# Turning b1's gradient ahead of the weight gradients, storing du later, and loading two tables behind more of w2: one change to a planned forward and backward kernel

## The chip, the cores and the metric

The kernel runs on one core of a Trainium2 chip. The metric is device time in microseconds; a run's time is that of its one core. The profile shows one execution, so every duration in it is a single sample.

## The reference

One layer of a token mixer and its gradients. With x of 2048 tokens by 448 channels:

```python
def _A_ref(x, w_r, w_i):                       # mixer
    X = rfft2(x) * (w_r + 1j * w_i)
    return irfft2(X, s=(S, D)).astype(bfloat16)

def _B_ref(x, w1, b1, w2, b2):                 # MLP over the tokens
    h = layernorm(x)
    u = gelu(einsum("bsd,sf->bdf", h, w1) + b1)
    return (einsum("bdf,fs->bds", u, w2) + b2).transpose(0, 2, 1)

h  = x + _A_ref(layernorm(x), w_r, w_i)
h2 = h + _B_ref(layernorm(h), w1, b1, w2, b2)
```

The outputs are h2 (out_0) and, for a given grad_out, the gradients of x (out_1), w_r and w_i (out_2, out_3), w1 (out_4, 2048x1792), b1 (out_5, 1792), w2 (out_6, 1792x2048) and b2 (out_7). S is 2048, D 448, F 1792; everything large is bf16.

## The kernel before

The kernel is written as a list of operations and ordered by a planner (class `Plan`). Each operation names the tiles it reads and writes, the engines that may run it with a planned duration, and, for a load, its place in SP's queue. `Plan.order` simulates the engines in time: at each step it takes the engine that can start earliest, and on it the ready operation with the highest priority. Priority is the longest chain of planned durations behind an operation, plus a boost (`pl.boost`, kept as `level`). An operation that may run on two engines goes to the one that is free first. Loads and stores pass through one modelled DMA server. The result is a fixed order per engine, and on the chip each engine runs its own list in order, waiting for semaphores.

The matrix products' banks are one ring of 8, with a limit per kind of use: "mm" 4, "mg" 2, "sp" 5, "sb" 4, "mw" 8, "mp" 6. A bank is taken when its first operation is placed, and comes free when the last reader is through.

The stages in order of time, with the names that the tiles have in the profile:

- Forward FFT over tokens and channels (`fft_rows`, `fft_cols`, banks `ps_sp`), the product with w (`cmul`), and the inverse (`ifft_cols`, `ifft_rows`). `ifft_cols` reads the table `hi`, of which VectorE first makes a negated part (L672); `ifft_rows` reads `di` and `kinv`.
- As filler between these, grad_out by w2 transposed: 14 blocks `w2T`, 16 matmuls each (`ps_mg<-go_n,w2T`), left in `du`. Blocks 0 and 1 of w2 are loaded plain and turned on TensorE (`turn`, L592), eight tiles to a bank, and copied out by ScalarE or VectorE, whichever the planner chooses; the others are loaded by a transposing DMA. The `w2T` tiles share the ring "w4" of five buffers.
- The products with w1 (`ps_mp<-hln,w1c`), 14 blocks of 16 matmuls. For each block ScalarE and VectorE make the GELU and its derivative; `gT` is the GELU, `du` becomes the gradient ahead of it, and `gb1` takes du's sums, one column per block. After every four blocks (L1103), gT and du are stored to `gT_d` and `du_d` in DRAM, from which they are later read back transposed. Stores go through GpSimd's queue.
- out_0: gT by w2 (`ps_mp<-gT,w2c`), boosted by 130.
- du by w1 transposed (`ps_mm<-du,w1T`), 16 blocks of 14 matmuls, each followed by `norm_back`. Meanwhile SP loads `g_t` and `goT` transposed (`ld_t4`: one load for the last 64+64 columns, one or two for the rest, and a copy within the tile through GpSimd's queue), then `w_b` (w again), `xr`, `hlnT` and `du_t`. `du_t` takes over du's place (X8).
- Backward FFT (`ps_sb`), with the gradient of w2 as filler: `outer("mm", g_t, goT, ...)`, 14 blocks of 16 matmuls, each with four banks of kind "mm". One block is: two groups `whole(0)` and `whole(1)` of three matmuls into one bank each, the `tails`, four matmuls on half the rows that touch all four banks, and `whole(2)` and `whole(3)`. Its four evictions on ScalarE (`s<-ps_mm`) are given priority 300.
- The gradient of w1, `outer` with hlnT and du_t: the first 6 of 16 blocks as filler in "mm" banks, the rest in "mw".
- b1's gradient at the end of the list: `gb1b` is gb1 cast to bf16, turned on TensorE (L1372) into a bank of kind "mm", copied out as `gb1r` and stored. It has no boost. Where it lands in time is the planner's choice.

SP's queue in the first stage, in order: x, the FFT's tables, w2 blocks 0 to 3, w_t (four loads), `hi`, `kinv`, `di`, `b1r`, `b2r`, then w2T 4 to 9, w1.

Of the kernel before, what the change touches and what calls it, by code (L numbers as in the profile page):

```python
# [12 lines left out]
BF16 = mybir.dt.bfloat16  # L13
# [5 lines left out]
P = 128  # L19
# [364 lines left out]
def on_act(n, base=0.045):  # L384
    return [("ACT", *_act(n, base))]
# [28 lines left out]
def kernel(  # L414
# [97 lines left out]
    def copy(alts, out, in_, r, w):  # L512
        def go(e, on):
            if on == "ACT":
                e.copy(out=out(), in_=in_())  # L515
            else:
                e.tensor_copy(out=out(), in_=in_())  # L517

        pl.op(alts, go, r=r, w=w)
# [32 lines left out]
    w2T = {}  # L552
    w2n = {}

    def ld_x(g):
        for i in range(4):
            pass
        sl = slice(4 * g, 4 * g + 4)
        ld_parts(x, range(4 * g, 4 * g + 4), lambda b: b[:, sl, :], xv[:, sl, :], P * 4 * D * 2)

    def ld_parts(dst, parts, out, in_, size, transpose=False, r=(), rate=None):
        place[0] += 1
        order = place[0]
        rate = rate or (0.195 if transpose else 0.335)

        def go(e, on):
            kw = {"transpose": True} if transpose else {}
            e.dma_start(out=out(dst), in_=in_() if callable(in_) else in_, **kw)

        pl.op([("SP", 0.45, 0.45)], go, r=r, w=[(dst, k) for k in parts], dma=(size, rate * 1e6, transpose), order=order)  # L570
# [15 lines left out]
    def turn(j, w2n):  # L586
        for a in range(0, NT, 8):
            pt = bank(sp[0], [P, 8, P], BF16)

            def go(e, on, a=a, pt=pt):  # L590
                for t in range(8):
                    e.transpose(pt[:, t], w2n[:, (a + t) * P:(a + t + 1) * P], ident[:])  # L592

            pl.op(mm(*[128] * 8), go, r=[w2n, ident], w=[pt])
            copy(on_act(1024) + [("DVE", 1.13, 1.21)], lambda a=a: w2T[j][:, a:a + 8, :], lambda pt=pt: pt[:], [pt], [(w2T[j], a)])
            turned.append(pl.ops[-1])

    turned = []
# [27 lines left out]
    ld_w2T(3)  # L626
    w_t = big(4, [P, 2, NJ, DF], "w_t")
    ld_w(w_t)
    hi = const("hi", [P, NJ, 3, 64])
    ld(hi, lambda b: b[:, :, 1:3, :], hnd["hi"].ap(), P * NJ * 2 * 64 * 2, w=(hi, 0))  # L630
    kinv = table("kinv", "kinv", [P, 3, P])
    di0 = table("di0", "di", [P, 2, 2, DC])
    b1r = const("b1r", [NFB, P])
    ld(b1r, lambda b: b[:], B_b1.rearrange("(j p) -> j p", p=P), 4000)
    b2r = const("b2r", [NT, P])
    ld(b2r, lambda b: b[:], B_b2.rearrange("(t p) -> t p", p=P), 4000)
    ld_w2T(4)
    ld_w2T(5)
    ld_w2T(6)
    ld_w2T(7)  # L640
    ld_w2T(8)
# [428 lines left out]
    for j in range(NFB):  # L1070
        wc, o = w1c[j]
        pu = product("mp", D, [(lambda wc=wc, o=o, h=h: wc[:, h, o:o + P], lambda h=h: hln[:, h, :],
                                [(wc, j), (hln, h)]) for h in range(NT)], [P, 512])
        ge = pl.buf("e4", [P, 4, D], "ge")
        uf, q_, zz, hh = 0, 1, 2, 3
        kk = zz

        def gop(alts, r, w, fn, ge=ge):
            pl.op(alts, lambda e, on: fn(e, lambda i: ge[:, i, :]), r=[(ge, k) if isinstance(k, int) else k for k in r],
                  w=[(ge, k) if isinstance(k, int) else k for k in w])  # L1080

        gop([("ACT", 0.516, 0.62)], [pu, b1c], [uf], lambda e, g, j=j, pu=pu: e.activation(
            out=g(uf), in_=pu[:, 0:D], func=ACT.Identity, bias=b1c[:, j:j + 1]))
        gop([("ACT", 0.516, 0.62)], [pu, b1q], [q_], lambda e, g, j=j, pu=pu: e.activation(  # L1084
            out=g(q_), in_=pu[:, 0:D], func=ACT.Square, bias=b1q[:, j:j + 1], scale=Q6))
        gop(stt, [q_, uf], [zz], lambda e, g: e.scalar_tensor_tensor(  # L1086
            out=g(zz), in0=g(q_), scalar=6.0 * GELU_C, in1=g(uf), op0=ALU.add, op1=ALU.mult))
        gop([("ACT", 0.475, 0.57)], [zz], [hh], lambda e, g: e.activation(
            out=g(hh), in_=g(zz), func=ACT.Sigmoid, scale=1.0 / 3.0))
        gop(bf_tt, [uf, hh], [(gT, j)], lambda e, g, j=j: e.tensor_tensor(  # L1090
            out=gT[:, j, :], in0=g(uf), in1=g(hh), op=ALU.mult))
        gop([("ACT", 0.475, 0.57)], [zz], [kk], lambda e, g: e.activation(
            out=g(kk), in_=g(zz), func=ACT.Sigmoid, scale=-1.0 / 3.0))
        gop(stt, [q_, uf], [q_], lambda e, g: e.scalar_tensor_tensor(
            out=g(q_), in0=g(q_), scalar=2.0 * GELU_C, in1=g(uf), op0=ALU.add, op1=ALU.mult))
        gop(bf_tt, [kk, q_], [kk], lambda e, g: e.tensor_tensor(out=g(kk), in0=g(kk), in1=g(q_), op=ALU.mult))
        gop(bf_tt, [hh, (du, j)], [hh], lambda e, g, j=j: e.tensor_tensor(
            out=g(hh), in0=g(hh), in1=du[:, j, 0:D], op=ALU.mult))
        gop([("DVE", 0.545, 0.69)], [kk, hh], [(du, j), (gb1, j)], lambda e, g, j=j: e.scalar_tensor_tensor(
            out=du[:, j, 0:D], in0=g(kk), scalar=1.0, in1=g(hh), op0=ALU.add, op1=ALU.mult,  # L1100
            accum_out=gb1[:, j:j + 1]))
        copy(small(), lambda j=j: du[:, j, D:D + 1], lambda j=j: gb1[:, j:j + 1], [(gb1, j)], [(du, (j, 1))])
        if j % 4 == 3 or j == NFB - 1:  # L1103
            j0 = j - j % 4
            js = range(j0, j + 1)
            st(lambda j0=j0, j=j: gT_v()[:, j0:j + 1, :], lambda j0=j0, j=j: gT[:, j0:j + 1, :],
               P * len(js) * D * 2, [(gT, k) for k in js], [(gT_d, j)])
            st(lambda j0=j0, j=j: du_v()[:, j0:j + 1, :], lambda j0=j0, j=j: du[:, j0:j + 1, 0:D],
               P * len(js) * D * 2, [(du, k) for k in js], [(du_d, j)])

# [70 lines left out]

    def norm_back(pb, xhat, xkey, h, nm, base, out, okey):


        nm2 = col(1, "nm2", bufs=3)
        ab = col(2, "nm1", bufs=3)  # L1190
        junk = pl.buf("jk", [P, D], "junk")
        v = pl.buf("f2", [P, D], "v", F32)

        def total(src, key, scale, r):
            pl.op([("DVE", 0.605, 0.73)], lambda e, on: e.tensor_tensor_reduce(  # L1195
                out=junk[:], in0=src[:, 0:D], in1=xhat(), scale=scale(), scalar=0.0, op0=ALU.mult,
                op1=ALU.add, accum_out=nm2[:]), r=[key, xkey] + r, w=[junk, nm2])

        def scaled():
            pl.op([("ACT", 0.53, 0.64)], lambda e, on: e.activation(  # L1200
                out=v[:], in_=pb[:, 0:D], func=ACT.Identity, scale=nm.rn[:, h, 0:1], bias=ab[:, 1:2]),
                r=[pb, ab, (nm.rn, (h, 0))], w=[v])

        if nm.rneg is not None:
            by, m = lambda: ab[:, 0:1], ab
            total(pb, pb, lambda: nm.rneg[:, h:h + 1], [nm.rneg])
            pl.op([("DVE", 0.075, 0.17)], lambda e, on: e.tensor_scalar(  # L1207
                out=ab[:], in0=nm.rn[:, h, :], scalar1=nm2[:], scalar2=None, op0=ALU.mult),
                r=[nm2, (nm.rn, (h, 0)), (nm.rn, (h, 1))], w=[ab])
            scaled()  # L1210
        else:
            by, m = lambda: nm2[:], nm2
            pl.op([("DVE", 0.131, 0.213)], lambda e, on: e.tensor_scalar(  # L1213
                out=ab[:, 1:2], in0=pb[:, D:D + 1], scalar1=nm.rn[:, h, 0:1], scalar2=-1.0 / D, op0=ALU.mult,
                op1=ALU.mult), r=[pb, (nm.rn, (h, 0))], w=[ab])
            scaled()
            total(v, v, lambda: nm.back, [])
        pl.op([("DVE", 0.595, 0.68)], lambda e, on: e.scalar_tensor_tensor(  # L1218
            out=junk[:], in0=xhat(), scalar=by(), in1=v[:], op0=ALU.mult, op1=ALU.add),
            r=[xkey, m, v, junk], w=[junk])  # L1220
        pl.op(tt(448), lambda e, on: e.tensor_tensor(out=out(), in0=junk[:], in1=base(), op=ALU.add),  # L1221
              r=[junk, okey[0]], w=[okey[1]])
# [14 lines left out]
    for h in range(8, NT):  # L1237
        ld_w1T(h)
        if h == 11:
            ld_t4(g_t, lambda: gT_d[:], [gT_d])  # L1240
    ld_t4(goT, lambda: grad_out[0], [], 2)
    dh = go_r
    for h in range(NT):
        pd = product("mm", D + 1, [(lambda h=h, j=j: w1T[h][0][:, w1T[h][1], j, :], lambda j=j: du[:, j, 0:D + 1],
# [121 lines left out]

    gb1b = const("gb1b", [P, NFB])
    copy(small(), lambda: gb1b[:], lambda: gb1[:], [gb1], [gb1b])  # L1370
    pt1 = bank("mm", [NFB, P], BF16)
    pl.op(mm(128), lambda e, on: e.transpose(pt1[:], gb1b[:], ident[:]), r=[gb1b, ident], w=[pt1])  # L1372
    gb1r = const2("b1r", [NFB, P], "gb1r")
    copy(small(), lambda: gb1r[:], lambda: pt1[:], [pt1], [gb1r])
    st(out_5.rearrange("(j p) -> j p", p=P), lambda: gb1r[:], 4000, [gb1r])
    gb2b = const("gb2b", [P, NT])
    copy(small(), lambda: gb2b[:], lambda: gb2[:], [gb2], [gb2b])
    st(out_7.rearrange("(q h) -> q h", h=NT), lambda: gb2b[:], 4000, [gb2b])
# [33 lines left out]
```

## Time and profile before

| | |
|---|---|
| median of 3 runs | 346.82 us (345.92 to 347.43) |
| the profiled execution | 345.45 us, span 343.7 us |
| granted TensorE clock | 0.997 |
| TensorE, matmul | busy 325.3 us (95%), 2507 instructions |
| TensorE, weight load | busy 174.3 us (51%) |
| VectorE | busy 269.1 us (78%) |
| ScalarE | busy 194.3 us (57%) |
| GpSimd | busy 70.9 us (21%), nearly all of it DMA issues |
| DMA | 80.98 MB, mean 236 GB/s |

The profiled execution's own time is its span and 1.75 us around it. Matmuls are pipelined and their ends are modelled, so short pauses of TensorE can hide in "busy". A bracket behind a line of the timeline gives the engine's idle time just before, and who ended it. ps_ names are banks, by kind.

### The profile page before, as it was taken

Reading aid. Unit: us, or ns where it says so; the run is one execution under the profiler, and the core shown is the slowest. Engines: PE = TensorE matmul, PEld = TensorE weight load, DVE = VectorE, ACT = ScalarE, POOL = GpSimd, SP = SyncE. Lnnn points to the kernel's source line nnn. Section 1 sums busy time; section 2 is a strip of 40 time slices with the busy share of each in tenths; the row PEclk is TensorE's granted clock in tenths of the full one; section 3 lists DMA queues with packets and bytes.
Section 4 is the critical chain, followed back from the end, with each engine's and each line's share of the span. In section 5 each row is a group of like instructions: output and inputs, shape, how many; then the busy total and the mean of one; then the engine's idle time right before and its main releaser. Section 6 shows DMA issues by size and latency. Waiting matters only on the chain. (4 is left out here: it accounts for less than half of the span.)

```text
span 343.7 us, 6872 instructions
## 1 busy us (share of the span) xinstructions
PE 325.3 (95%) x2507; PEld 174.3 (51%) x2507; DVE 269.1 (78%) x756; ACT 194.3 (57%) x416; POOL 70.9 (21%) x125
## 2 busy tenths in 40 slices
PE   0979999999999999999999999889999999999994
PEld 0546555666655555555555555544445655544441
DVE  5898999897649997060267887869999799999773
ACT  2897833476568773616012322687876888665332
POOL 0000000056520101040340000010111133336553
PEclk9999999999999999999999999999999999999998
DMA  7999699979799999899969999999999466556756
GB/s 255 383 241 209 143 189 260 221 202 292 216 333 262 355 306 317 249 331 244 217 121 269 201 212 232 240 203 199 211 200 200 181 232 230 196 201 215 254 202 201
DMA packets 134845, 80.98 MB, mean 236 GB/s; under 512 B 94332, under 2 KB 127228, under 8 KB 134684
## 3 DMA queue, kind: packets, MB, share of 16 engines
q1 hardware_dynamic: 127180, 52.71, 71.4%
q0 software_dynamic: 7632, 27.84, 22.7%
q8 instruction: 19, 0.31, 0.5%
q14 instruction: 14, 0.11, 0.1%
HBM read 30.98 MB, written 27.08 MB: 169 GB/s over the span
## 5 line engine op out<-in xcount | busy, mean ns | idle before, releaser
L525 PE MATMUL ps_mg<-go_n,w2T 128*128 128x448 bf16 x224 | 49.9, 355 | 1.6 <-DMA go_n<-in_grad_out_dram 0.8
L525 PE MATMUL ps_mm<-goT,g_t 128*128 128x512 bf16 (+1 forms) x224 | 50.4, 380 | 0.4 <-DVE zt L517 0.4
L515 ACT CAST s<-ps_mm 128x512 bf16<-128x512 f32 (+1 forms) x72 | 38.8, 584 | 8.2 <-PE ps_mm L525 7.5
L525 PE MATMUL ps_mm<-du,w1T 128*128 128x449 bf16 x224 | 43.3, 353 | 0.0
L525 PE MATMUL ps_mp<-hln,w1c 128*128 128x448 bf16 x224 | 43.0, 352 | 0.0
L525 PE MATMUL ps_mp<-gT,w2c 128*128 128x448 bf16 x224 | 42.7, 352 | 0.0
L1200 ACT ACTIVATE v<-ps_mm,nm,rn_h 128x448 f32<-128x448 f32 x16 | 11.6, 724 | 43.9 <-DVE nm L1213 43.9
L525 PEld LDWEIGHTS <-w1T 128*128 128x128 bf16 x224 | 21.8, 97 | 21.1
L525 PEld LDWEIGHTS <-w2c 128*128 128x128 bf16 x224 | 21.9, 98 | 20.5
L525 PEld LDWEIGHTS <-w1c 128*128 128x128 bf16 x224 | 21.8, 98 | 20.1
L525 PEld LDWEIGHTS <-hlnT 128*128 128x128 bf16 (+1 forms) x256 | 19.9, 97 | 23.6 <-issue 7.8
L507 POOL DMA_DIRECT2D out_dram<-s x31 | 17.0, 547 | 54.2 <-ACT s L515 34.7
L525 PEld LDWEIGHTS <-w2T 128*128 128x128 bf16 x224 | 19.3, 98 | 17.3 <-issue 1.7
L525 PE MATMUL ps_mw<-du_t,hlnT 128*128 128x448 bf16 (+1 forms) x160 | 27.7, 353 | 0.0
L525 PEld LDWEIGHTS <-g_t 128*128 128x128 bf16 (+1 forms) x224 | 15.4, 96 | 20.1 <-issue 8.5
L1173 DVE SCALAR_TENSOR_TENSOR h<-ps_mp,b2c,hr 128x448 bf16<-128x448 f32 x16 | 9.9, 676 | 19.8 <-PE ps_mp L525 19.8
L515 ACT CAST s<-ps_mw 128x448 bf16<-128x448 f32 x21 | 10.7, 534 | 16.3 <-PE ps_mw L525 12.2
L1086 DVE SCALAR_TENSOR_TENSOR ge<-ge 128x448 bf16<-128x448 bf16 x14 | 8.7, 619 | 14.0 <-ACT ge L1084 14.0
L525 PE MATMUL ps_mm<-du_t,hlnT 128*128 128x448 bf16 (+1 forms) x96 | 18.0, 353 | 0.0
L525 PEld LDWEIGHTS <-kinv 128*128 128x128 bf16 x192 | 14.6, 97 | 6.4 <-DVE eo L951 2.4
L1180 ACT ACTIVATE gb2j<-go_r 128x448 bf16<-128x448 bf16 x16 | 9.2, 576 | 15.0 <-DMA go_r<-in_grad_out_dram 14.6
L507 POOL DMA_DIRECT2D hn_d<-x x4 | 2.4, 599 | 73.0 <-DVE mv_h L719 73.0
(148 smaller groups left out, 602.4 us busy)
## 6 DMA issues: line engine op xcount, KB each, us to landing
w2c<-in_B_w_dram SPq DMA_DIRECT2D x8, 896.0 KB, 8.8
out_dram<-s POOLq DMA_DIRECT2D x14, 512.0 KB, 5.9
out_dram<-s POOLq DMA_DIRECT2D x15, 448.0 KB, 2.9
w1c<-in_B_w_dram SPq DMA_DIRECT2D x6, 1024.0 KB, 10.0
x<-in_A_x_dram SPq DMA_DIRECT2D x4, 448.0 KB, 6.6
go_n<-in_grad_out_dram SPq DMA_DIRECT2D x2, 896.0 KB, 10.3
hn_d<-x POOLq DMA_DIRECT2D x4, 448.0 KB, 6.2
hln_d<-hln POOLq DMA_DIRECT2D x4, 448.0 KB, 6.1
```

The lines of the kernel that those rows point to most:

```text
L507: e.dma_start(out=out() if callable(out) else out, in_=in_())
L515: e.copy(out=out(), in_=in_())
L525: e.matmul(out(), lhsT=lhsT(), rhs=rhs(), start=start, stop=stop)
L1086: gop(stt, [q_, uf], [zz], lambda e, g: e.scalar_tensor_tensor(out=g(zz), in0=g(q_), scalar=6.0 * GELU_C, in1=g(uf), op0=ALU.add, op1=ALU. ...
L1173: pl.op([("DVE", 0.595, 0.68)], lambda e, on, t=t, p2=p2, h2=h2: e.scalar_tensor_tensor(out=h2[:], in0=p2[:, 0:D], scalar=b2c[:, t:t + 1], ...
L1180: pl.op([("ACT", 0.70, 0.80)], lambda e, on, h=h: e.activation(out=gb2j[:], in_=go_r[:, h, :], func=ACT.Copy, accum_out=gb2[:, h:h + 1]), ...
L1200: pl.op([("ACT", 0.53, 0.64)], lambda e, on: e.activation(out=v[:], in_=pb[:, 0:D], func=ACT.Identity, scale=nm.rn[:, h, 0:1], bias=ab[:, ...
```

## The change

Four edits, and one line that only rewrites `ld_x` (the same four loads).

1. The four operations for b1's gradient move from the end of the list to the place behind out_0 and b2's sums, with a boost of 130, and the bank's kind becomes "mg".
2. du's four stores leave the GELU loop and stand behind the loads of goT; each is made to wait for the last of those loads. `pl.ops[-2]` is that load: the last operation of `ld_t4` is the copy within the tile.
3. On SP, w2T 4 goes ahead of kinv, di, b1r and b2r, and `hi` goes behind w2T 5.
4. The planned duration of VectorE's copy of a turned block of w2 goes from 1.13 (to completion 1.21) to 0.62 (0.70). ScalarE's stays at 0.92.

```diff
-            copy(on_act(1024) + [("DVE", 1.13, 1.21)], lambda a=a: w2T[j][:, a:a + 8, :], ...
+            copy(on_act(1024) + [("DVE", 0.62, 0.70)], lambda a=a: w2T[j][:, a:a + 8, :], ...
...
     ld_w(w_t)
-    hi = const("hi", [P, NJ, 3, 64])
-    ld(hi, lambda b: b[:, :, 1:3, :], hnd["hi"].ap(), P * NJ * 2 * 64 * 2, w=(hi, 0))
+    ld_w2T(4)
     kinv = table("kinv", "kinv", [P, 3, P])
...
-    ld_w2T(4)
     ld_w2T(5)
+    hi = const("hi", [P, NJ, 3, 64])
+    ld(hi, lambda b: b[:, :, 1:3, :], hnd["hi"].ap(), P * NJ * 2 * 64 * 2, w=(hi, 0))
     ld_w2T(6)
...
-            st(lambda j0=j0, j=j: du_v()[:, j0:j + 1, :], lambda j0=j0, j=j: du[:, j0:j + 1, 0:D],
-               P * len(js) * D * 2, [(du, k) for k in js], [(du_d, j)])
...
+    pl.boost = 130.0
+    gb1b = const("gb1b", [P, NFB])
+    copy(small(), lambda: gb1b[:], lambda: gb1[:], [gb1], [gb1b])
+    pt1 = bank("mg", [NFB, P], BF16)
+    pl.op(mm(128), lambda e, on: e.transpose(pt1[:], gb1b[:], ident[:]), r=[gb1b, ident], w=[pt1])
+    gb1r = const2("b1r", [NFB, P], "gb1r")
+    copy(small(), lambda: gb1r[:], lambda: pt1[:], [pt1], [gb1r])
+    st(out_5.rearrange("(j p) -> j p", p=P), lambda: gb1r[:], 4000, [gb1r])
+    pl.boost = 0.0
...
     ld_t4(goT, lambda: grad_out[0], [], 2)
+    behind = pl.ops[-2]
+    for j0 in (0, 4, 8, 12):
+        js = range(j0, min(j0 + 4, NFB))
+        st(lambda js=js: du_v()[:, js[0]:js[-1] + 1, :], lambda js=js: du[:, js[0]:js[-1] + 1, 0:D],
+           P * len(js) * D * 2, [(du, k) for k in js], [(du_d, js[0])])
+        pl.ops[-1].deps.add(behind.idx)
...
-    gb1b = const("gb1b", [P, NFB])
...
-    pt1 = bank("mm", [NFB, P], BF16)
...
```

## The prediction

> **What bounds the kernel now.** I read the page first. TensorE is busy for 95% of the span at full granted clock, and its slices show no hole between the first two and the last that a tenth would reveal, apart from one stretch past the middle.
>
> ```profile
> PE 325.3 (95%) x2507; PEld 174.3 (51%) x2507; DVE 269.1 (78%) x756; ACT 194.3 (57%) x416; POOL 70.9 (21%) x125
> ...
> PE   0979999999999999999999999889999999999994
> ...
> DMA  7999699979799999899969999999999466556756
> ```
>
> So a change pays where TensorE stands still, or where its own instructions become fewer. This change removes no arithmetic. I therefore listed the idle time of TensorE by stretches (first number in each line: width; second: TensorE busy). Of 18.4 us idle in the span, 8.0 lie ahead of the first operand, some 5 after the last matmul, 2.6 between 8 and 30 us, and 2.9 in one place, 218 to 226 us:
>
> ```profile
> 214.00:218.00 4.00, 4.00 (x31) 2.34 (x30) 2.57 (x8) 1.16 (x3) 0.00 (x0) 1.00 1.12 259
> 218.00:222.00 4.00, 3.06 (x31) 1.86 (x28) 3.96 (x11) 3.13 (x7) 0.00 (x0) 1.00 1.01 233
> 222.00:226.00 4.00, 2.07 (x32) 1.92 (x32) 3.34 (x12) 3.42 (x8) 0.52 (x1) 1.00 0.99 213
> 226.00:230.00 4.00, 4.00 (x50) 1.99 (x48) 2.04 (x6) 3.58 (x10) 0.57 (x1) 1.00 1.20 250
> ```
>
> The timeline of that place shows why (columns: start, duration, engine, line, operation, and in brackets the idle time before it and who ended it):
>
> ```profile
> 218.35 0.22 PE L1372 MATMUL ps_mm<-ident,gb1b 128*14 128x128 bf16 x1
> ...
> 219.80 0.81 PE L525 MATMUL ps_mm<-goT,g_t 128*128 128x512 bf16 x3 [0.41 <-DVE zt L517]
> ...
> 220.66 0.81 PE L525 MATMUL ps_mm<-goT,g_t 128*128 128x512 bf16 x3
> ...
> 222.56 1.10 PE L525 MATMUL ps_sb<-kf,w 128*113 128x128 bf16 x16 [1.08 <-DVE w L517]
> ...
> 224.86 0.20 DVE L517 COPY gb1r<-ps_mm 14x128 bf16<-14x128 bf16 x1
> 225.03 0.96 PEld L525 LDWEIGHTS <-w 128*113 128x113 bf16 x16 [1.51 <-DVE w L517]
> 225.03 1.10 PE L525 MATMUL ps_sb<-kf,w 128*113 128x128 bf16 x16 [1.37 <-DVE w L517]
> ...
> 226.07 2.01 PE L525 MATMUL ps_mm<-goT,g_t 64*128 64x512 bf16 x10
> ```
>
> At 218.35 b1's gradient is turned (L1372) into a bank of kind "mm", of which the planner allows four at once. VectorE copies it out only at 224.86, because that copy has the lowest priority. The first block of out_6 has run two of its four groups of three matmuls (219.80, 220.66), one bank each, and its next step, the tails, writes all four banks of the block: the fourth is the one that holds the turned gradient. TensorE then waits 1.08 and 1.37 us for the FFT's folds, with filler at hand that has no bank. As soon as the copy is out, the remaining ten matmuls of the block run (226.07).
>
> After this place TensorE has no visible hole until its last block: the chain that ended last closes with it.
>
> ```profile
> 311.65 25.12 PE ps_mw L525 x147
> ```
>
> What is won at 222 us therefore comes out at the end, unless another wait opens.
>
> **The gradient's turn.** It moves ahead of out_6, into kind "mg", at a boost of 130. Its input is ready early: the last du ends at 148.8 on VectorE, and the cast to gb1b ran at 152.34 even without boost. The turn ranks below every product of out_0 (by the planner's rule theirs is 130 plus at least 3.5, the turn's 130 plus 2.6) and above the du by w1T products, so I expect it right after out_0's last product, about 177.5. Cost: the same 0.22 us matmul, the same 0.24 and 0.205 us copies and the 0.52 us store, only elsewhere. VectorE has room there (it idles 10 us before 162.55), so I take zero; if TensorE had to wait for the cast, the price would be that 0.24.
>
> Gain: the ten matmuls take 226.07 to 228.00, 1.93 us, and now fit into the 2.45 us of waiting. The group at 219.80 also waited 0.41 us for a bank; with one more free I take half, 0.2. Together 2.1. Ends: 2.86 (all three waits) and nothing (all given back, the first rival).
>
> **du's stores.** Four issues on GpSimd (three of 0.75, one of 0.72, 3.0 in all) leave 113 to 150 us, where no engine waited for what they delayed, so no gain. They now wait for the last load of goT: issued 210.3, landing 6.1 later, 216.4. Queued behind them on GpSimd are the stores of out_6 (first at 229.0) and two copies within hlnT and du_t (240.9, 260.5). GpSimd idled 14.8 us up to 225.35, so 3.0 us from 216.4 to 219.4 hold nobody up: zero.
>
> Their 1.61 MB (14x128x448 x 2 bytes) now compete with SP's loads. At the lowest rate of the stretches shown, 213 GB/s, that is 7.5 us. Who is hit: w_b, whose last part is issued about 216.9 and takes 10.1 us, so lands at 227.0; VectorE first needs it at 236.04. Wholly behind du's stores it lands at 234.5, still 1.5 us early. hlnT and du_t are needed at 291.4, while the last of them lands at 269.3 (260.52 plus 8.8): 22 us of cover. du's slot is refilled by du_t, which now also waits for du's stores to land: about 219.4 plus 6.8 is 226.2, and that load starts at 239.17. I take zero; what hides it is w_b's cover of 9.0 us, and without it the 7.5 would stand on VectorE's path. The first line is from the list of DMA issues, the second from VectorE's timeline:
>
> ```profile
> w_b<-in_A_w_i_dram SPq DMA_DIRECT2D x2, 450.0 KB, 10.1
> ...
> 236.04 1.08 DVE L868 TENSOR_TENSOR t_r<-ds,w_b 128x1800 bf16<-128x1800 bf16 x1
> ```
>
> The engines are full there (DMA share 0.99 to 1.20 in the stretches above), and no row shows how two queues divide them. The Trainium skill says, in "DMA: Bandwidth & Descriptors", section "Queues, rings and completion order", that each engine switches between the queues after every packet, so du's stores would not wait behind w_b but slow it. By that the sum would be minus 1.0 and not minus 2.1 (the third rival).
>
> **The inverse columns' tables.** hi moves behind w2T 4 and 5 on SP, kinv and its neighbours behind w2T 4. Three lines of SP's timeline, and one of VectorE's:
>
> ```profile
> 24.95 0.61 SPq L501 DMA_DIRECT2D hi<-tab_hi  x1
> 25.60 8.87 SPq L501 DMA_DIRECT2D kinv<-tab_kinv  x1
> ...
> 37.20 16.29 SPq L501 DMA_TRANSPOSE w2T<-in_B_w_dram  x6
> ...
> 48.56 0.41 DVE L672 TENSOR_SCALAR hi<-hi 128x1024 bf16<-128x1024 bf16 x1
> ```
>
> Now hi is issued at 24.95, lands 11.9 later (36.9), and is first read at 48.56, when VectorE negates it; the columns' matmuls follow at 49.02. One block of w2T costs SP 16.29/6, 2.7 us, and lands in about 5.5. SP is stuck on kinv until 34.5, behind w_t's small packets. If w2T 4 is issued within that stuck time, hi follows one block later than SP's present 37.2, at 39.9; if not, two blocks later, at 42.6. To landing it takes between 5.5 (a w2T behind a w2T) and 11.9 (its own row, which stood behind w_t's 10.9). So it lands between 45.4 and 54.5: from in time to 5.9 late. I take in time, about 47, since what stands ahead of it is a w2T and no longer w_t. On the other side, w2T 4 comes sooner; but in the list of waits TensorE's weights waited only 0.4 us in the whole run for any w2T, and TensorE's idle from 30 to 50 us is 0.2. Gain at most 0.4, taken as zero. b1r shifts by about one block less hi: from about 38.5 to 40, with its turn at 42.05.
>
> **The planner's figure** for evicting a turned block of w2 on VectorE falls from 1.13 to 0.62. All four evictions ran on ScalarE (1.01 us each). The planner gives them to the engine that is free first and not to the quicker one; the figure enters only as 0.21 less priority. I take no move. If one went to VectorE, it would cost between its 0.68 row for 512 columns and twice that, with up to 1.0 off ScalarE: plus 1.4 to minus 1.0. ld_x is only rewritten.
>
> All these feed one list planner, so the order of filler and FFT steps on TensorE can shift anywhere. TensorE's weight loads idle 32.4 us in 94 places without a named cause, 0.34 each; three such places more or fewer are plus or minus 1.0.
>
> **Sum.** Minus 2.1, all else zero. The profiled run took 345.45 (span 343.7 and 1.75 around it), which becomes 343.35. The median of the runs shown is 346.82, 1.37 above it; for the median I forecast 344.7. A measurement here can tell about 0.5%, 1.7 us, from no change.
>
> **Rivals.**
>
> *Given back to the FFT (0.22).* out_6's four evictions (2.21 us on ScalarE) carry the top priority. Moved to 222 us, they meet a ScalarE that is copying zt without pause from 219.86 to 225.08, so the column transform starts up to 2.2 us after 228.0. From 229 to 313 VectorE is nearly always busy, and TensorE's order is fixed, so its FFT instructions may wait instead. For it: ScalarE's and VectorE's load. Against: out_6 and out_4 give filler up to 311.5, some 3.6 after the last FFT matmul (307.5 to 307.9). It would leave 0 to 1.2 of the gain: 345.6 to 346.8, say 346.3.
>
> *The turn doesn't open the bank (0.04).* If the planner binds the fourth bank otherwise, the waits stay: 346.8.
>
> *w_b slowed (0.07).* If du's stores take every other packet, w_b's 10.1 us can double: it lands at 237.1, 1.1 after its first use. That leaves 1.0 of the gain: 345.8. For it: full engines. Against: w_b is issued from 215.1 to 217.5, so part of it has landed before the stores begin at 216.4.
>
> *hi late (0.14): slower.* If hi lands after 48.56, VectorE stands at the negation and TensorE, in order, at 49.02. VectorE is busy without a gap from 38 to 64, so each microsecond is lost to the chain, and the fill by w2T ends at 88.9 in any case. The case outweighs the gain from a landing at 50.7 on, and is slower by over 0.5% from 52.4. At its bound (54.5) the time is 350.6; I place the case at 349.5. For it: hi's own row of 11.9. Against: the reason for that row, w_t's backlog, has drained by then.
>
> **How the numbers follow.** The forecast holds 0.53: 344.7, its own range 343.0 (2.86 instead of 2.1, and 1.0 of order) to 345.1. Rivals within 0.5% hold 0.22, 0.04 and 0.07, in all 0.33; slower is 0.14. The range reaches from 343.0 to 347.5, which takes in the first three rivals with 0.7 of order above 346.8, and leaves out hi's case and the edges.
>
> **What would show it.** Right: no gb1r copy after 200 us; between 218 and 226 TensorE idle falls from 2.9 us below 1, with "x4" tails of 64 rows before the third group of folds; the start of the "ps_mw" matmuls moves from 311.5 to about 309.4. du's stores stand between 216 and 220 on GpSimd, and VectorE's first product with w_b is not preceded by a wait for a DMA. Wrong: a wait of VectorE's L672 or of TensorE's "hi" matmuls near 49 us; the FFT's column steps beginning after 230 us; new idle time of TensorE at "ps_sb" between 229 and 310; or ScalarE no longer doing four w2T copies.

## The result: slower by 2.7%

| | before | after |
|---|---|---|
| median, all executions | 347.12 us (6) | 361.21 us (6) |
| range | 345.92 to 363.53 | 355.04 to 371.06 |
| ratio after to before | | 1.0267, 95% interval 1.0212 to 1.0322 |
| the profiled execution | 345.45, span 343.7 | 360.76, span 359.0 |

The forecast was 344.7 us, at most 347.5. One thing is needed to read the numbers: executions of one kernel spread here, and the ratios compare only the undisturbed ones (355.04 and 357.15 for after), so the profiled execution of after, which is not one of them, lies some 5 us above what the ratio speaks of.

The page of after: TensorE's busy time and its slices, its granted clock, the DMA engines' busy share, and the moved GB/s.

```profile
PE 327.4 (91%) x2494; PEld 175.8 (49%) x2507; DVE 267.4 (74%) x750; ACT 196.8 (55%) x422; POOL 71.0 (20%) x125
...
PE   0989999999999999999999997399997599999993
...
PEclk9999999999999999999999999699999699999998
DMA  7999999996999999999999999999999998645756
GB/s 241 383 225 196 175 194 277 174 266 216 304 285 326 277 256 271 251 270 222 211 237 186 199 193 156 188 194 158 152 191 119 192 273 302 213 192 192 256 196 217
```

Before had one stretch below 9 tenths past the middle; after has two deep ones (slices 25 and 26, then 31 and 32), and in each the clock falls. The span grew by 15.3: TensorE's busy time by 2.1 (327.4 against 325.3), its idle time by 13.2. The places of that idle time, from windows: 218 to 230 us 7.4 instead of 2.9, 240 to 300 us 7.2 instead of 0.2; the rest is 1.7 at the two ends. The windows at the first place (width, then busy time of TensorE, weight loads, VectorE, ScalarE, GpSimd; granted clock, DMA share, GB/s):

```profile
214.00:218.00 4.00, 4.00 (x24) 2.12 (x23) 2.49 (x8) 1.03 (x2) 0.00 (x0) 1.00 1.20 190
218.00:222.00 4.00, 3.59 (x42) 2.43 (x40) 3.96 (x11) 3.27 (x7) 0.00 (x0) 1.00 1.14 163
222.00:226.00 4.00, 0.88 (x12) 0.76 (x13) 3.62 (x11) 2.91 (x6) 0.00 (x0) 1.00 1.35 99
226.00:230.00 4.00, 0.11 (x1) 0.10 (x1) 0.00 (x0) 0.00 (x0) 0.00 (x0) 0.60 0.86 198
230.00:234.00 4.00, 4.00 (x16) 1.80 (x15) 0.69 (x1) 1.17 (x2) 0.05 (x1) 0.54 1.09 232
```

From 218 to 230 us the DMA engines are at a share of up to 1.35 and move 99 to 198 GB/s; before it was 213 to 250. The timeline there names what TensorE waited for:

```profile
208.21 0.53 POOL L507 DMA_DIRECT2D goT<-goT  x1 [20.39 <-DMA goT<-in_grad_out_dram]
...
208.72 2.99 POOL L507 DMA_DIRECT2D du_d<-du  x4
...
221.03 0.61 PE L525 MATMUL ps_mm<-goT,g_t 64*128 64x512 bf16 x4
...
222.63 0.88 PE L525 MATMUL ps_sb<-kf,w 128*113 128x128 bf16 x12 [1.00 <-DVE w L517]
...
229.89 1.44 PE L525 MATMUL ps_mm<-goT,g_t 128*128 128x512 bf16 x3 [6.38 <-DMA goT<-in_grad_out_dram]
...
231.12 0.63 PE L525 MATMUL ps_sb<-kf,w 128*113 128x128 bf16 x4
...
236.06 1.02 PE L525 MATMUL ps_sb<-df,zt 113*64 113x113 bf16 x32
```

GpSimd sends du's four stores at 208.72, right behind the copy within goT (which needs an earlier part of goT), when goT's third load has just been issued: some 8 us before the prediction let them start. TensorE then waits 6.38 us for goT, the FFT's step at 231.12 stands behind it in TensorE's order, and the column transform (236.06) begins 6 us beyond the 230 that the prediction gave as its alarm. DMA issues (count, KB each, median us from issue to landing); before, in the order of the lines, 5.9, 6.8, 6.1, 13.1 and 24.2:

```profile
out_dram<-s POOLq DMA_DIRECT2D x14, 512.0 KB, 13.1
...
du_d<-du POOLq DMA_DIRECT2D x3, 448.0 KB, 19.3
...
goT<-in_grad_out_dram SPq DMA_TRANSPOSE x3, 6.5
...
hlnT<-hln_d SPq DMA_TRANSPOSE x2, 30.7
du_t<-du_d SPq DMA_TRANSPOSE x2, 12.9
```

goT's row is the median of three; its third load, issued at 208.6, took 21.3. SyncE's queue shows what follows. The second number is how long the queue was held by the loads of that line:

```profile
233.59 42.89 SPq L566 DMA_TRANSPOSE hlnT<-hln_d  x2
276.72 15.39 SPq L566 DMA_TRANSPOSE du_t<-du_d  x2
292.22 18.57 SPq L566 DMA_DIRECT2D xr<-in_A_x_dram  x5
```

Before, these lines began at 221.81, 239.17 and 274.59, and hlnT held the queue for 17.13.

### The profile page after: what moved, and what is told of

Read it like the earlier page. It is cut to its first block, busy times and chain, and to the rows that moved or that the text cites. A ratio compares the mean times of both kernels' runs of the same rounds, so it can differ in the third digit from the quotient of the medians.

```text
span 359.0 us, 6850 instructions
## 1 busy us (share of the span) xinstructions
PE 327.4 (91%) x2494; PEld 175.8 (49%) x2507; DVE 267.4 (74%) x750; ACT 196.8 (55%) x422; POOL 71.0 (20%) x125
## 4 chain that ended last, share of the span: by engine, by line
PE 70%; issue 12%; DMA 11%; POOL 2%; DVE 2%; SPq 1%; ACT 0%; POOLq 0%; DVEq 0%; ACTq 0%
PE ps_mp L525 24%; PE ps_mm L525 17%; PE ps_mg L525 11%; PE ps_sp L525 8%; DMA out_dram<-s 6%; PE ps_mw L525 6%; PE ps_sb L525 4%; DMA go_n<-in_grad_out_dram 2%; DMA goT<-in_grad_out_dram 2%; POOL out_dram L507 1%; POOL du_d L507 1%; SPq L566 1%; DMA out_dram<-gw 1%; DVE bs_x L687 1%; DVE u L776 0%
## 5 line engine op out<-in xcount | busy, mean ns | idle before, releaser
L525 PE MATMUL ps_mm<-goT,g_t 128*128 128x512 bf16 (+1 forms) x211 | 52.0, 398 | 8.1 <-DMA goT<-in_grad_out_dram 6.4
L515 ACT CAST s<-ps_mm 128x512 bf16<-128x512 f32 (+1 forms) x74 | 40.3, 585 | 17.9 <-PE ps_mm L525 15.6
L525 PEld LDWEIGHTS <-g_t 128*128 128x128 bf16 (+1 forms) x224 | 16.3, 100 | 27.9 <-issue 17.3
L515 ACT CAST s<-ps_mw 128x448 bf16<-128x448 f32 x24 | 11.7, 539 | 14.6 <-PE ps_mw L525 14.2
## 6 DMA issues: line engine op xcount, KB each, us to landing
out_dram<-s POOLq DMA_DIRECT2D x14, 512.0 KB, 13.1
```

The source lines that it names most:

```text
L525: e.matmul(out(), lhsT=lhsT(), rhs=rhs(), start=start, stop=stop)
```

## What the experiments had to tell apart

The first theory: du's stores run beside goT's transposing load, because `deps.add(behind.idx)` orders the planner's list and makes no wait on the chip. The rival: the planner's new order of all engines. Later a second term of the loss came up, with rivals of its own. Unless the text says "planned afresh", a kernel has the order of its parent on every engine and only the named operations moved.

### du's stores alone, and all but du's stores

On the order of before, du's stores moved behind goT's copy:

```diff
     pl.order()
+    pl.done = [o for o in pl.done if o not in du_st]
+    at = pl.done.index(goT_copy) + 1
+    pl.done[at:at] = du_st
     pl.emit()
```

> The order of before on every engine, to the instruction, with one difference: du's four stores are taken out of GpSimd's list at 113 to 149 us and put right behind the copy within goT (210.0 in before), which is where they stood on the chip in the changed kernel. Theory 1 (the stores are sent while goT's last transposing load is still in flight, and slow it and the loads behind it): the last goT load lands in about 20 us and not 6.1, TensorE waits 5 to 7 us for it near 221, and the time is 353 to 357, 7 to 10 above before. Rival (the new order of the planner, not the stores, makes the changed kernel slow): within 1.5 us of before, 345.5 to 348.5, with the goT load at 6 to 8 us.

Measured: 358.21 us median of 4, ratio 1.0243 (1.0162 to 1.0324). GpSimd's and TensorE's timeline:

```profile
215.40 3.00 POOL L507 DMA_DIRECT2D du_d<-du  x4
...
234.11 2.29 PE L525 MATMUL ps_mm<-goT,g_t 128*128 128x512 bf16 x5 [4.52 <-DMA goT<-in_grad_out_dram]
```

goT's slow load took 18.9 us. A second long wait of TensorE, 5.50 us up to 293.6, was for one of out_6's evictions on ScalarE, which itself waited for a store of out_6 to land.

The reverse: the changed kernel's order, each of du's stores back beside the gradient's store.

```diff
+    pl.done = [o for o in pl.done if o not in du_st]
+    for i in range(4):
+        at = max(pl.done.index(gT_st[i]), pl.done.index(du_op[i])) + 1
+        pl.done.insert(at, du_st[i])
```

> The order of the changed kernel on every engine, to the instruction, with du's four stores put back behind gT's stores (110 to 149 us). Theory 1: goT's last load lands in about 6 us again, TensorE's waits near 224 and 277 us go, and the time is that of the prediction without its error, 344 to 346. Rival (the planner's new order): still 352 or more.

Measured: 347.71 us median of 10, ratio 1.0011 (0.9972 to 1.0050). So the moved stores make the whole loss, whichever order they are put into, and the rival falls. The gain that the other edits were to bring does not show either; that comes below.

### A real wait

GpSimd reads the last columns of goT ahead of the stores, so that they really follow its last load:

```diff
+    wait.fn = lambda e, on: e.tensor_scalar(out=gate[:], in0=goT[:, 0, S - 4:S], ...)
+    pl.done.insert(min(pl.done.index(o) for o in du_st), wait)
```

> The order of the changed kernel with one instruction added on GpSimd ahead of du's stores: a 128x4 operation that reads the end of goT, so that the stores are sent only when goT's last load has landed, as the prediction took it. If the missing wait alone is the cause: stores from about 215, goT's last load at 6 to 7 us, 345 to 347. If the stores' traffic behind goT also costs (w_b, hlnT and du_t later, and TensorE's wait near 277 us stays): 348 to 353. If the rival (order) holds: 352 or more.

Measured: 361.99 us median of 4 (352.94 to 370.76; too scattered for a ratio). goT's loads landed in 6.0 us in the median and 7.3 at most, and the wait for goT was gone, as expected; but the time was not back. VectorE's wait (us in total, times, longest; `junk` is the scratch output of the step that reads xr), and the lines of SyncE's queue behind it:

```profile
DVE junk L1203 <- DMA xr<-in_A_x_dram: 15.4, 1, 15.4
```

```profile
246.52 37.76 SPq L566 DMA_TRANSPOSE du_t<-du_d  x2
284.38 25.21 SPq L566 DMA_DIRECT2D xr<-in_A_x_dram  x5
```

The second group of xr stands behind du_t's transposing loads on SyncE; they held the queue until 284.3, and VectorE, with TensorE behind it, stood for 15 us. The theory that the missing wait is the whole cause is refuted. Beside the wait for goT (the first term) there is a second one: hlnT and du_t hold SyncE too long.

### Other places and another queue for du's stores

Two of the four stores early, two behind goT's copy:

```diff
-    for i in range(4):
+    for i in range(2):
         ...
+    at = pl.done.index(goT_copy) + 1
+    pl.done[at:at] = du_st[2:]
```

> The changed kernel with every engine's order as it is, but two of du's four stores (0.92 MB) go out beside the gradient's stores again, and only the last two (0.69 MB) behind goT's copy. If the loss grows with the bytes that lie in the stretch from 208 us on, about 0.43 of the 9.3 us that moving all four costs is left: 350 to 353 us, with goT's third load landing in 10 to 14 us. If it is a matter of having any store beside the transposing loads, nearly all of it is left: 354 us or more, goT at 16 us or more. If only a long jam hurts, because the folds' cover of some 9 us swallows a short one: 347 to 349 us.

Measured: 345.23 to 357.2 in 4 executions, median 352.89. goT's slowest load took 12.5, hlnT and du_t held SyncE for 31.8 and 25.5, and VectorE waited 10.1 for xr. The median and goT's load are in the ranges of "grows with the bytes", but the executions reach from below the lowest of the three ranges into the highest, so this settles nothing on its own.

All four behind b1's gradient's store, near 178 us:

```diff
+    at = pl.done.index(gb1_st) + 1
+    pl.done[at:at] = du_st
```

> The changed kernel's order, with all four of du's stores right behind b1's gradient's store, near 179 us on GpSimd, where TensorE has 30 us of out_6's products ahead. Both theories (stores slow the transposing loads beside them; the bytes are late) expect the stretch from 210 us on to be as with the stores beside the gradient's: goT's third load in 6 to 7 us, and 346 to 349 us. They differ at 180 to 200 us: if stores slow transposing loads wherever they meet, g_t's loads (8.4 us from issue to landing) and w1T's (6.0 us) take 15 us or more, TensorE waits for w1T there by some us, and the time is 349 to 354 us; if it is only bytes, both are later by at most 7 us, which w1T's lead over its readers takes up, and nothing is lost.

Measured: 358.38 us median of 10, ratio 1.0098 (1.0029 to 1.0167). g_t's loads held SyncE for 13.1 instead of 8.6 us there, less than expected, and TensorE did not wait for w1T; the stretch from 222 on was again the late one (hlnT 34.2, then a wait of 4.2 for xr). So the stores cost TensorE nothing where they stand, as the theory of late bytes had it, and the end is later all the same, which neither theory had.

All four on SyncE's queue, behind goT's last load:

```diff
+    for o in du_st:
+        o.on = "SP"
+    at = pl.done.index(goT_last) + 1
+    pl.done[at:at] = du_st
```

> The changed kernel's order, with du's four stores on SyncE's queue behind goT's last load instead of on GpSimd's, so that they share a queue with the transposing loads. If the loss comes from two queues being served in turn (stores and transposes side by side), goT lands in 6 to 7 us, the stores take 7 to 8 us, df, w_b and what follows are later by some 5 to 7 us, which w_b's cover of 9 us takes up, and the time is 346 to 350 us. If it is the bytes alone, in a stretch whose transfers are already the bound (hlnT's and du_t's transposes end at the same time as their readers want them), these are later by 7 us or more whichever queue carries the stores, out_6's stores are slow as in the run with a real wait (14.8 us), and the time is 352 to 360 us.

Measured: 366.1 us median, ratio 1.0542 (1.0436 to 1.0649): the largest ratio of all, and beyond both expectations. goT was unhurt (6.2 in the median, 7.6 at most) and the stores took 3.9. SyncE's queue:

```profile
213.89 3.46 SPq L507 DMA_DIRECT2D du_d<-du  x4
...
224.19 39.79 SPq L566 DMA_TRANSPOSE hlnT<-hln_d  x2
264.08 22.35 SPq L566 DMA_TRANSPOSE du_t<-du_d  x2
286.55 23.11 SPq L566 DMA_DIRECT2D xr<-in_A_x_dram  x5
```

du's stores were through, yet hlnT, issued 2.4 us later than before, held the queue for 39.8 us instead of 17.1. So serving two queues in turn is not the whole of it. What runs beside hlnT and du_t in every kernel so far is out_6's stores, 512 KB each.

### out_6's stores in strips

The stores carry only the first 32 of out_6's 2048 columns, 8 KB instead of 512 KB each, and the rest of out_6 is left out. First in the changed kernel:

```diff
-        st(out_6[j * P:(j + 1) * P, :], lambda s6=s6: s6[:], P * S * 2, [s6])
+        st(out_6[j * P:(j + 1) * P, 0:32], lambda s6=s6: s6[:, 0:32], P * S * 2, [s6])
```

> The changed kernel, whose out_6 stores carry only the first 32 of 2048 columns (8 KB instead of 512 KB each; the rest of out_6 is left out); every engine's order is as it was. In the changed kernel hlnT's and du_t's transposing loads held SyncE's queue for 42.9 + 15.4 us, while out_6's blocks were stored beside them. If these stores slow the transposing loads, both together hold SyncE for 20 to 35 us, the second group of xr goes out by 280 us instead of 292, TensorE's stall of 5.7 us at the tenth product of hi and w_b is gone or under 2 us, and the wait for goT near 224 (6.4 us), which comes before any store of out_6, stays: a span of 348 to 353 us. If the loads are slow for another reason (what du's stores left behind, or their own 64 KB of 2-byte elements), they hold SyncE for 50 us or more and the span is 356 us or more.

Measured: span 342.8 in the profile, below the expected range; 344.56 to 352.58 us in 4 executions. SyncE's queue:

```profile
226.47 15.68 SPq L566 DMA_TRANSPOSE hlnT<-hln_d  x2
242.39 9.18 SPq L566 DMA_TRANSPOSE du_t<-du_d  x2
275.86 18.77 SPq L566 DMA_DIRECT2D xr<-in_A_x_dram  x5
```

The holds fell from 58.3 to 24.9 us and xr went out by 276. goT's slow load stayed (17.0 us; 21.3 in the profile of after), but TensorE waited only 0.6 for it in this execution, the shortest of the four. The other three were at 350 to 352.6; that it is the first term that makes them longer is likely and not shown.

With both edits, the real wait and the strips, both terms are taken away:

> The kernel with the real wait, whose out_6 stores carry only the first 32 of 2048 columns (the rest of out_6 is left out). Two terms are taken to make the whole loss: goT's transposing load beside du's stores (taken away by the real wait), and hlnT's and du_t's transposing loads beside out_6's stores, which du's stores push into each other (taken away by the strips). If that is all, neither a wait for goT nor one for xr is left, hlnT and du_t hold SyncE for 20 to 35 us together (62.8 with the real wait alone), and the time is 343 to 347 us. If du's 1.61 MB cost something of their own behind goT, a wait of 3 us or more is left (w_b, hlnT, du_t or xr) and the time is 349 us or more.

Measured: 343.91 us (343.65 to 345.24 in 5), ratio 0.9923 (0.9899 to 0.9947). Windows and queue:

```profile
218.00:226.00 8.00, 7.01 (x77) 4.81 (x75) 7.96 (x23) 7.50 (x15) 0.58 (x1) 1.00 1.00 301
240.00:250.00 10.00, 10.00 (x111) 4.94 (x110) 8.36 (x19) 7.92 (x19) 1.11 (x2) 1.00 1.10 192
250.00:260.00 10.00, 10.00 (x109) 4.72 (x107) 9.34 (x22) 7.67 (x16) 1.08 (x2) 1.00 0.02 3
```

```profile
221.60 15.23 SPq L566 DMA_TRANSPOSE hlnT<-hln_d  x2
237.06 10.38 SPq L566 DMA_TRANSPOSE du_t<-du_d  x2
```

By 250 us the transposing loads are over (the DMA engines' share is 0.02 from 250 to 260), though du's stores still go out behind goT. So the two terms together are the loss. Whether the 0.8% below before is the strips' own is told by the same strips in the kernel before:

> The kernel before, whose out_6 stores carry only the first 32 of 2048 columns (the rest of out_6 is left out); every engine's order is as it was. It is the control of the run with a real wait and strips (0.9923 of the time before). If that gain is the gradient's turn, whose 1.9 us at 218 to 226 us only show once the transposing loads are undisturbed, the kernel before gains less than 0.3% by the strips: 346 to 347 us. If it is the strips alone, the kernel before with strips is at 0.990 to 0.994, some 344 us. In both, hlnT and du_t hold SyncE for 20 to 30 us (38.5 in before), and no execution is above 348 us.

Measured: 346.91 us median of 12 (345.77 to 348.11), ratio 1.0009 (0.9987 to 1.0031). The strips alone gain nothing, so the changed plan does gain once its transposing loads are undisturbed: 0.9923 against 1.0009 is 0.9%, 3.0 us (two rounds, each against its own runs of before). The strips also took most of the spread away in these two kernels (1.6 and 2.3 us, against 8.8 and 21.2 us for before beside them); with the strips and no real wait it was 8.0.

### How the second term becomes lost time

With the real wait, xr's second group on GpSimd:

```diff
+    for o in xr_op:
+        o.on = "POOL"
```

> The kernel with the real wait, whose second group of xr (five loads of 224 KB) is issued by GpSimd at the planned places instead of by SyncE behind du_t's loads. In the run with the real wait, du_t's loads held SyncE until 284.3 us, VectorE then waited 15.4 us for xr and TensorE 15.0 us behind it. If that queue order is what turns late transposes into lost time, the wait for xr falls under 3 us and the span from 358.1 to 344 to 350 us. If the transfers themselves are the bound there, the wait moves to du_t or to the stores' buffers, and the span stays at 354 us or more.

Measured: 353.69 us median, ratio 1.0192 (1.0140 to 1.0244), wait for xr 8.6. Wait and span (352.4) lie between the two expectations: du_t's copy, ahead of xr on GpSimd, itself stood 16.0 us there, until du_t's load had landed. With that copy behind the third xr:

```diff
+    pl.done.remove(du_copy)
+    pl.done.insert(pl.done.index(xr_op[2]) + 1, du_copy)
```

> As the kernel whose second group of xr is issued by GpSimd behind a real wait, but du_t's copy, which held GpSimd for 16.0 us there until du_t's load had landed, now stands behind the third of xr's five loads on that queue. If it is the place in a queue behind a late transposing load that turns it into lost time, VectorE's wait for xr (15.4 us with xr on SyncE, 8.6 us behind the copy) falls under 2 us and the span is 345 to 350 us. If the stores and loads there are late for their own traffic, or the stores' buffers run out, TensorE keeps waits of 5 us or more near 280 to 297 and the span stays at 352 us or more.

Measured: 344.82 to 381.9 us in 10 executions, median 358.8. Four lay at 344.8 to 349.1, and their ratio is 0.9962 (0.9893 to 1.0030); six lay at 357.7 to 381.9. The profiled one, the longest, had a span of 380.1. Its DMA issues:

```profile
out_dram<-s POOLq DMA_DIRECT2D x14, 512.0 KB, 18.0
...
xr<-in_A_x_dram POOLq DMA_DIRECT2D x5, 224.0 KB, 18.6
...
du_t<-du_d SPq DMA_TRANSPOSE x2, 50.3
```

There xr, issued by another queue (the first load at 277.5), took 18.6 us, and du_t 50.3: with the place in the queue taken away, the loads themselves were late. The four short executions are what the theory of the queue's order expected, and with the real wait alone none of four was under 352.9; but no trace shows them, and the long ones are what the rival expected. So the place in the queue is one way in which late transposing loads reach VectorE, and not the only one.

### The other edits alone

The gradient's turn alone (the change's two hunks with gb1b), planned afresh:

> Before with edit 1 alone, planned anew: b1's gradient turned behind out_0 in a bank of kind mg. The prediction's own term: the first block of out_6 is through by about 224, TensorE's idle time from 218 to 226 falls from 2.9 below 1, and the time is 1.5 to 2.5 below before (344 to 345.5). Rival (given back to the FFT): 0 to 1 below before.

Measured: 346.76 us median of 10, ratio 0.9986 (0.9953 to 1.0018). The two waits for the FFT's folds, 1.07 and 1.37, were still there, with the block's tails now ahead of both of them.

The tables and the planner's figure alone (its hunks with hi and 0.62), planned afresh, twice:

> The kernel before with the third and fourth edits alone: the inverse columns' tables behind two more blocks of w2, and the planner's figure for w2T's copies. The theory that du's stores make the whole loss expects no change: 346 to 348 us, hi landing before VectorE's first reading of it near 48.6 us. The rival, hi late, expects VectorE to wait at that reading and a time above 348.5 us.

> The tables' edit alone a second time, beside the same runs of before as the change without its second edit: if its gain is real, 0.992 to 0.996 of the time before; if the first measurement was a chip's mood, 0.998 to 1.002.

Measured: 0.9936 (0.9914 to 0.9958), then 0.9985 (0.9953 to 1.0017): no loss. The second does not confirm the gain of the first. With the planner's figure alone, the program that comes out is that of before, to the byte.

The change without the hunk that moves du's stores, planned afresh:

> The change without its second edit (du's stores back beside the gradient's stores), planned afresh: the gradient's turn early, and the tables behind two more blocks of w2. If the parts add, it gains what the runs of the parts alone showed (0.9986 and 0.9936 of the time before): 0.992, some 344 us. If the order that starts out_6 earlier takes it back by slower transposes, as in the run with the changed order and early stores (1.0011), it is at 346.5 to 348 us, within 0.3% of before.

Measured: 346.37 us median of 12, ratio 0.9975 (0.9937 to 1.0013), within 0.3% of before, as the second expectation had it, and not at the 0.992 of the first; the two waits for the folds (2.4) remain in this plan too.

### A version that was to keep the gain

The changed order, du's stores early, and out_6's first stores held behind hlnT's copy:

```diff
+    at = pl.done.index(hlnT_copy)
+    held = [o for o in pl.done[:at] if o in out6_st]
+    pl.done = [o for o in pl.done if o not in held]
+    at = pl.done.index(hlnT_copy) + 1
+    pl.done[at:at] = held
```

> The changed kernel's order with du's stores early (347.71, 1.0011 of before), and in addition out_6's first four stores held on GpSimd until hlnT's transposing load has landed (they stand behind hlnT's copy; the ring of five tiles lets TensorE go on). If transposes beside stores are what eats the gain of 1.9 us at 218 to 226 us, hlnT holds SyncE for 16 us or less and lands near 236, du_t is the only one left beside the stores, both together hold it for 45 us or less (53.1 without the hold), and the time is 343.5 to 346 us, with fewer long executions. If the four stores, let go together, jam du_t's load by as much as they spared hlnT's, or the fifth tile's eviction waits for a store's landing, the time is 346.5 to 350 us.

Measured: 344.96 to 359.49 in 6 executions, median 352.28, no gain. hlnT held SyncE for 12.0 us instead of 16.7, but du_t for 39.8 instead of 36.4: the second of the two mechanisms expected, with a median above its range.

## Why the prediction was wrong, by its steps

**du's stores, "I take zero"** is the step that failed, by some 9 us, and in three places.

- *"They now wait for the last load of goT"*, and the same in the second edit's description: false. The dependence only orders the planner's list. The stores went out at 208.7, not 216.4, into goT's third load.
- *Who is hit*: I named w_b and gave it its cover. It did nearly double, landing 19.1 us after its issue instead of 10.1. (The rule that I had cited from the Trainium skill, "DMA: Bandwidth & Descriptors", section "Queues, rings and completion order", that engines switch between queues after every packet, agrees with that.) But nobody waited for w_b, whose first reading had itself moved from 236.0 to 242.1. goT, a load already under way ahead of the stores, was hit (21.3 us instead of 6.1), and TensorE with it.
- *"1.61 MB at 213 GB/s is 7.5 us"* and "22 us of cover" for hlnT and du_t: a volume divided by a rate. This is the part that counts most, since the time was not back with the real wait. The transposing loads behind the stores lost far more than 7.5 us: with the real wait they held SyncE for 62.8 us against 38.5. And xr, queued behind them with some 14 us in hand (du_t's hold ended at 260.6 before, xr went out at 274.6), was not in my list of who is hit.

**The gradient's turn, minus 2.1**: the mechanism was right, and its condition was missed. In after the turn runs right after out_0:

```profile
176.29 0.22 PE L1186 MATMUL ps_mg<-ident,gb1b 128*14 128x128 bf16 x1
...
177.64 0.20 DVE L517 COPY gb1r<-ps_mg 14x128 bf16<-14x128 bf16 x1
```

I had said 177.5 and nothing from TensorE. The tails, four products on 64 rows, stand ahead of the third group of folds in after (221.03 against 222.63), as forecast. In the plan of the whole change, where goT is in time, the idle time at 218 to 226 is 1.0 us (the window 218 to 226 of the run with wait and strips, 7.01 of 8) instead of 2.9: 1.9 of the 2.1. But planned alone the bank was free too, and the planner put ten of the block's products ahead of both waits and none between them, so both waits stayed: a free bank is needed for the gain and is not enough. And where the gain was made (changed order, stores early), out_6's first store left 4.3 us after hlnT's issue instead of 7.2, and hlnT and du_t held SyncE for 53.1 instead of 38.5; that the earlier stores cause this is what the strips suggest, not shown by itself. In that run's profile TensorE stood 2.67 us in a stop that before does not have (it is told of at the end), more than the 1.9 us won. "given back to the FFT", my likeliest rival at 345.6 to 346.8, is near the time of that run (347.7) and not of the change; the stop is not its mechanism.

**The tables, zero**: right. The forecast was a hi issued at 39.9, landing at about 47 and read in time; it landed 6.2 us after its issue, at 46.0:

```profile
39.80 0.60 SPq L501 DMA_DIRECT2D hi<-tab_hi  x1
```

```profile
48.85 0.41 DVE L670 TENSOR_SCALAR hi<-hi 128x1024 bf16<-128x1024 bf16 x1
```

"hi late", the only slower rival, had the right sign for a wrong reason. **The planner's figure**: right, four copies still on ScalarE.

**"ps_mw" from 311.5 to 309.4**: wrong for after. Its chain closes with

```profile
325.86 20.79 PE ps_mw L525 x122
```

and with the same 122 matmuls from 309.01 in the run with wait and strips: 16.9 us earlier, and near the 309.4 (before, the block that began at 311.65 had 147 matmuls, so the mark is not quite the same).

## What to carry to other kernels

A dependence given to a planner is a wish about order; look for what makes the chip wait before costing a transfer as "behind" another. Do not price a transfer that is put beside transposing loads by its bytes: look which of them are under way, what stands behind them in the same queue, and how much that has in hand. Moving filler forward moves its stores forward too; look what they meet there (that this took the gain back here is suggested and not shown).

## What the runs showed of the hardware

- hlnT's and du_t's transposing loads and out_6's stores in flight together are slow together. With strips, these loads were done by 250 to 252 us, at 192 to 220 GB/s in the window 240 to 250; with out_6's full stores beside them they went on until 284 to 292 in after, with the real wait, and with the stores on SyncE, at as little as 69 GB/s with the DMA engines at a share of 1.25. The Trainium skill's "Advanced Engine Details and Errata", section "X-Bar Transpose (TRN2)", says that transposing DMAs are as fast as plain ones. Here plain traffic ran at 333 to 341 GB/s (92 to 104 us, changed order with early stores), so the trace does not bear that out for these loads beside these stores. It is not so wherever the two meet: in the same run four transposing loads of w1T (from 117 and from 133 us) went out beside 448 KB stores of gT and du, in windows of 302 and 345 GB/s (117 to 127, 133 to 142), and took 9.2 and 7.5 us from issue to landing, against 5.9 in the median of all of w1T's loads. What makes the difference is open.
- TensorE's granted clock fell within some 4 us of standing still: 0.60 and 0.54 at 226 to 234 above, 0.63 and 0.52 at the second place, so a wait costs more than its length (three products of goT and g_t took 1.44 us after the first wait, 0.81 before it). In windows of 1 us, it was 0.66 at 226.5 to 227.5 and 0.50 behind that, some 3 us after the last product ended at 223.5; in the second place it was still 1.00 at 277 to 278 and 0.51 in the next, some 2 us after the last product ended at 275.9. The Trainium skill, "TensorE: Matmul & The Clock Gate", section "Part 1: The HAM clock gate", says half rate after at least one idle window of about 3.4 us; the first place is near that, and in the second the clock fell sooner. The windows at the second place:

```profile
273.00:277.00 4.00, 2.90 (x35) 1.43 (x33) 2.83 (x8) 1.69 (x4) 0.53 (x1) 1.00 1.25 69
277.00:281.00 4.00, 0.00 (x0) 0.00 (x0) 0.00 (x0) 0.00 (x0) 0.00 (x0) 0.63 1.28 108
281.00:285.00 4.00, 3.08 (x15) 1.29 (x16) 1.18 (x3) 2.19 (x5) 0.00 (x0) 0.52 1.10 285
```

- At that second place every engine stood, and TensorE waited for nothing that the profile names:

```profile
275.41 0.49 PE L525 MATMUL ps_sb<-hi,w_b 64*113 64x128 bf16 x10
281.58 0.57 PE L525 MATMUL ps_sb<-hi,w_b 64*113 64x128 bf16 x6 [5.68 <-issue]
```

The same stop, at the same instruction (behind the tenth of sixteen products of hi and w_b), was 5.60 us in the run with the stores on SyncE, 2.67 with the changed order and early stores, and 1.37 with held stores, where an earlier group of these products stood for another 2.38. The trace lists a queue named "instruction" with 19 packets and 0.31 MB, 16 KB each; over about 5,000 matmuls and weight loads that would be some 60 bytes each, and one of these packets ran at 277.7, within the stop. That TensorE ran out of instructions, because their fetch stood behind the jammed transfers, is argued from this and not shown.

Left open: why du's stores, which had landed by some 228 us in the run with the real wait and by some 191 us where they stood behind b1's gradient, still left hlnT's loads longer on SyncE (25.0 and 34.2 us instead of 17.1) when out_6's stores were full, and why single executions of one kernel differ by up to 37 us there.
